# Transformer block on one core: the FFN of token-tile pairs computes silu and product for two inner blocks at once, under a new instruction order

## The chip, the core and the metric

The kernel runs on one core of a Trainium2 chip. The core has five engines with a queue each: TensorE (PE in the profile; its weight loads, which overlap the matmuls, are listed as PEld), VectorE (DVE), ScalarE (ACT), GpSimd (POOL) and SyncE (SP). SP issues nearly all DMA transfers here. The engines meet through semaphores. TensorE writes its results to PSUM, which has 8 banks of 512 fp32 columns by 128 partitions; DVE and ACT read them from there. The metric is the device time of one execution in microseconds, lower is better.

## The reference, cut to what matters

```python
x = A_x                                                # 1 x 2048 x 512, bf16
sa, ca, ga, sb, cb, gb = (silu(c) @ w_mod) in six parts of 512
h = layernorm(x) * (1 + ca) + sa
q, k, v = h @ wqkv, 32 heads of 16
# token s attends to tokens s, s-2, s-4, ..., s-14 (8 of them; those before 0 are masked)
x = x + ga * (softmax(q . k * 16**-0.5) weighted sum of v) @ wo
h = layernorm(x) * (1 + cb) + sb
x = x + gb * ((silu(h @ w1) * (h @ w3)) @ w2)          # 512 -> 1792 -> 512
```

The last line is the FFN, and the change is in it.

## The kernel before

**Tiles.** The 2048 tokens are 16 tiles of 128 (T = 0 to 15). All weights are loaded to SBUF once. Layernorm and the projections to q, k and v run over groups of 2, 2, 4, 4 and 4 tiles. v is written to a scratch tensor in DRAM and read back as eight shifted copies per tile (`vsh`, four DMAs a tile, into one of three buffers; the third, `vshx`, lies over the memory of `wqkv`, so it can be used only when all projections are done).

**Attention.** Per tile, DVE multiplies q with eight shifted views of k (line 742), TensorE sums these products into logits by small matmuls on a 128 x 32 tile of the array (line 752), DVE and ACT make the softmax, TensorE transposes the weights (line 807), DVE multiplies them with the shifted v (line 827), TensorE sums again by matmuls on a 128 x 32 tile (line 855), ACT copies the result (line 861), a DMA transposes it (`sb_ot`), TensorE multiplies it with wo (line 867), and DVE adds it to x (line 871).

**Second layernorm.** Sums of squares and the normalised tile are made on ACT (lines 590 and 601) with three small GpSimd instructions between them (lines 596 to 599). The first two groups of tiles are transposed on TensorE, the others by DMA (`sb_h`). ACT applies scale and shift (lines 644 and 621).

**FFN.** The tiles are taken in groups, `FFN = [[0,1],[2,3],[4,5,6,7],[8,9,10,11],[12,13],[14,15]]`. For a group, with `n` = 256 or 512 tokens, the inner width of 1792 is 14 blocks of 128. `ffn_unit` makes one block: 4 matmuls for the gate (w1) into one PSUM bank, silu on ACT into a buffer `tmp` (line 889), 4 matmuls for up (w3) into a second bank, and the product on DVE into a buffer `hh` (line 892). The matmuls of both are on line 883. For a pair of tiles, a block fills 256 of the 512 columns of each of its two banks. `ffn_w2` then takes the 14 `hh` blocks of a tile through w2 into one bank, 7 blocks and then 7 (line 921), or for the last two tiles in two halves of 256 columns, blocks 0 to 9 and then 10 to 13 (line 909); DVE adds x (line 931) and SP stores. w2 is first multiplied by gb on DVE in four groups of blocks (line 952).

**What sets the order.** `_build` lists operations with what they read and write. Each one's place is then fixed by two lists at the end of the file: `ORDER` gives the global order, from which every engine's own queue follows (SP's with its DMAs too), and `SLOTS` gives the PSUM bank or buffer of each value. Where an operation needs a value of another engine or of a DMA, or a buffer still held by an earlier value, its queue waits on a semaphore. Nothing is reordered at run time: a waiting operation holds all that follows on its engine. There are 20 `hh` buffers, 6 `tmp` buffers and 8 banks, shared by all stages. The costs `c_mm`, `c_act`, `c_dve` in the operations served the making of the lists, and do nothing in the running program.

Of the kernel before, what the change touches and what calls it, by code (L numbers as in the profile page):

```python
# [10 lines left out]
P = 128  # L11
# [261 lines left out]
def _build(p, A_x, A_wqkv, A_wo, B_w1, B_w3, B_w2, c, w_mod, out):  # L273
# [602 lines left out]
    def ffn_unit(gi, n, fi, vh, after):  # L876
        g = group_of[fi]
        k = ("f", NF * gi + fi)
        vgp, vup = Val("ps_g", psum), Val("ps_u", psum)

        def mm(e, vp, wt):
            for t in range(KT):
                ins = e.matmul(bank(vp)[:, 0:n], wt[:, t, fi * P:(fi + 1) * P], vh.at[:, t, 0:n], start=(t == 0),  # L883
                               stop=(t == KT - 1))
            return ins

        vt, vh_ = Val("tmp", tmppool), Val("hh", hhpool)
        o = p.op("pe", lambda e: mm(e, vgp, w1), 4 * c_mm(n), k, r=[vh, vw1[g]], w=[vgp], after=after)
        p.op("act", lambda e: e.activation(vt.at[:, 0:n], bank(vgp)[:, 0:n], ACT.Silu), c_act(n), k, r=[vgp], w=[vt],  # L889
             table="silu")  # L890
        p.op("pe", lambda e: mm(e, vup, w3), 4 * c_mm(n), k, r=[vh, vw3[g]], w=[vup], after=[o])
        p.op("dve", lambda e: e.tensor_tensor(vh_.at[:, 0:n], vt.at[:, 0:n], bank(vup)[:, 0:n], ALU.mult), c_dve(n), k,  # L892
             r=[vt, vup], w=[vh_])
        return vh_
# [4 lines left out]
    def ffn_w2(T, tt, vhh, zops):  # L899

        if T >= NT - 2:
            n = D // 2
            for q in range(2):
                vz = Val("ps_z", psum)
                o = None
                for a, c in ((0, 10), (10, NF)):
                    def mm(e, q=q, vz=vz, a=a, c=c):
                        for fi in range(a, c):
                            ins = e.matmul(bank(vz)[:, 0:n], vhh[fi].at[:, tt * P:(tt + 1) * P], w2[:, fi, q * n:(q + 1) * n],  # L909
                                           start=(fi == 0), stop=(fi == NF - 1))  # L910
                        return ins

                    o = p.op("pe", mm, (c - a) * c_mm(n), ("z", 2 * T + q), r=vhh[a:c] + vw2s[0 if a == 0 else 2:3 if a == 0 else 4], part=[vz], after=[o] if o else [])
                store(T, q * n, n, vz)
            return
        vz = Val("ps_z", psum)
        o = None
        for q in range(2):
            def mm(e, q=q):
                for fi in range(7 * q, 7 * q + 7):  # L920
                    ins = e.matmul(bank(vz), vhh[fi].at[:, tt * P:(tt + 1) * P], w2[:, fi, :], start=(fi == 0),  # L921
                                   stop=(fi == NF - 1))
                return ins

            o = p.op("pe", mm, 7 * MM, ("z", 2 * T + q), r=vhh[7 * q:7 * q + 7] + vw2s[2 * q - (q > 0):2 * q + 2], part=[vz], after=[o] if q else [])
            zops[q].append(o)
        store(T, 0, D, vz)
# [34 lines left out]
    zold = []  # L962
    for gi, Ts in enumerate(FFN):
        vns = [v for pr in pairs(Ts) for v in ln_sums(pr)]
        vh = ln_T(1, gi, vns)
        spare = NHH - NF
        vhh = [ffn_unit(gi, len(Ts) * P, fi, vh, zold if fi < spare else zops[0] if fi < spare + 7 else zops[1]) for fi in range(NF)]
        zold, zops = zops[1], [[], []]
        for tt, T in enumerate(Ts):
            ffn_w2(T, tt, vhh, zops)  # L970
# [106 lines left out]
```

## Time and profile before

| | us |
|---|---|
| median of 3 runs | 239.71 (237.94 to 240.3) |
| the profiled execution: its time | 239.43 |
| its span, first to last instruction | 237.7 |
| PE busy | 229.7 (97%) |
| DVE busy | 179.4 (75%) |
| ACT busy | 138.5 (58%) |
| POOL busy | 29.2 (12%) |
| DMA, share of 16 engines | 67% |
| FFN gate and up matmuls (line 883), busy | 53.0 with 256 columns, 49.9 with 512 |
| FFN down matmuls (lines 921 and 909), busy | 44.0 and 6.3 |

How to read it: a busy time is the union of an engine's instruction times. Matmuls are pipelined, so a matmul's row is longer than the step to the next one, and a TensorE that is busy by its rows may still have lost part of that time; where the text speaks of a step, it is the distance of the starts. A few matmul records are missing in the trace (25 of those on lines 691, 711, 867, 883 and 921). A line of a group gives engine, operation, output <- input, shapes and count, then busy time, mean duration in ns, and the engine's idle time before these instructions with what ended it. A line of the order in time gives start, duration, engine, line, operation and, in brackets, the idle time before it. `sb_hh` is `hh`, `sb_sg` is `tmp`, `pall` is PSUM, `sb_w` stands for w1, w2 and w3 together.

### The profile page before, as it was taken

To read this page: it belongs to the slowest core of one execution; us is meant where nothing else is said; L and a number is where in the kernel's file an instruction comes from. 1 tells how busy PE (TensorE), PEld (TensorE's weight loads), DVE (VectorE), ACT (ScalarE), POOL (GpSimd) and SP (SyncE) were. 2 spreads that over 40 slices of the span, in tenths; PEclk is the share of its full clock that TensorE was granted. 3 is DMA by queue.
4 is the path that set the end of the run, shared out by engine and by line. 5 is a ranking of instruction groups with operands and counts; after the bars stand their busy time and mean duration, and the time that the engine had idled before them with its cause. 6 is when DMAs were issued, how large, how long until landed. Compare 5 with 4: busy or idle time off the path is not lost.

```text
span 237.7 us, 4535 instructions
## 1 busy us (share of the span) xinstructions
PE 229.7 (97%) x1781; PEld 136.2 (57%) x1806; DVE 179.4 (75%) x279; ACT 138.5 (58%) x267; POOL 29.2 (12%) x66
## 2 busy tenths in 40 slices
PE   7999999999999998999999999999999999999995
PEld 4776454445588674664444444444475457485774
DVE  5699999999999989999999999682654403434433
ACT  2289577999978744985865594837473405040300
POOL 4434100013002000240002520012010000000000
PEclk9999999999999999999999999999999999999999
DMA  6999999999999999897981693642203000000202
GB/s 216 372 337 322 158 237 299 208 269 283 353 200 270 243 249 199 173 260 177 247 234 47 182 234 72 154 132 46 67 19 91 3 0 0 6 19 0 70 0 88
DMA packets 46317, 38.85 MB, mean 163 GB/s; under 512 B 21704, under 2 KB 37080, under 8 KB 46296
## 3 DMA queue, kind: packets, MB, share of 16 engines
q1 hardware_dynamic: 46288, 38.56, 66.9%
q8 instruction: 14, 0.23, 0.4%
q14 instruction: 7, 0.06, 0.1%
q10 hardware_dynamic: 8, 0.00, 0.0%
HBM read 29.62 MB, written 4.21 MB: 142 GB/s over the span
## 4 chain that ended last, share of the span: by engine, by line
PE 74%; DMA 8%; DVE 8%; SPq 4%; ACT 3%; issue 2%; ACTq 0%; DVEq 0%
PE pall L883 38%; PE pall L921 18%; DMA sb_x<-in_A_x_dram 5%; PE pall L867 5%; SPq L124 4%; PE pall L691 4%; DMA sb_vsh<-v_scratch_dram 3%; PE pall L909 3%; PE pall L855 2%; PE pall L752 2%; PE pall L711 2%; DVE sb_vsh L827 2%; DVE sb_pq L742 2%; DVE sb_hh L892 1%; ACT sb_h L621 1%
## 5 line engine op out<-in xcount | busy, mean ns | idle before, releaser
L883 PE MATMUL pall<-sb_h,sb_w 128*128 128x256 bf16 (+1 forms) x664 | 101.9, 307 | 1.8 <-DVE sb_hh L892 0.9
L883 PEld LDWEIGHTS pall<-sb_h,sb_w 128*128 128x128 bf16 x672 | 64.8, 98 | 37.2 <-issue 2.8
L889 ACT ACTIVATE sb_sg<-pall 128x256 bf16<-128x256 f32 (+1 forms) x84 | 35.6, 453 | 54.1 <-PE pall L883 53.0
L892 DVE TENSOR_TENSOR sb_hh<-sb_sg,pall 128x256 bf16<-128x256 bf16 (+1 forms) x84 | 39.9, 505 | 34.8 <-PE pall L883 32.7
L921 PE MATMUL pall<-sb_w,sb_hh 128*128 128x512 bf16 x190 | 44.0, 379 | 0.3
L742 DVE TENSOR_TENSOR sb_pq<-sb_q,sb_kT 128x4096 bf16<-128x4096 bf16 x16 | 36.3, 2282 | 0.0
L921 PEld LDWEIGHTS pall<-sb_w,sb_hh 128*128 128x128 bf16 x196 | 19.0, 98 | 21.6 <-DVE sb_hh L892 0.4
L691 PE MATMUL pall<-sb_h,sb_wqkv 128*128 128x512 bf16 (+1 forms) x154 | 30.2, 335 | 0.5 <-issue 0.2
L827 DVE TENSOR_TENSOR sb_vsh<-sb_vsh,sb_al 128x4096 bf16<-128x4096 bf16 x12 | 27.3, 2287 | 2.1 <-DMA sb_vsh<-v_scratch_dram 2.1
L621 ACT ACTIVATE sb_h<-sb_h,sb_modc 128x512 bf16<-128x512 bf16 (+1 forms) x24 | 16.5, 743 | 10.1 <-DMA sb_h<-sb_xn 10.1
L691 PEld LDWEIGHTS pall<-sb_h,sb_wqkv 128*128 128x128 bf16 x160 | 14.7, 98 | 11.8 <-ACT sb_ac L861 0.4
L931 DVE TENSOR_TENSOR sb_o<-pall,sb_x 128x512 bf16<-128x512 f32 (+1 forms) x18 | 11.1, 625 | 10.5 <-PE pall L921 6.8
L711 PE MATMUL pall<-sb_wqkv,sb_h 128*128 128x512 bf16 x62 | 15.5, 379 | 0.2
L867 PE MATMUL pall<-sb_wo,sb_ot 128*128 128x512 bf16 x61 | 15.3, 379 | 0.3 <-issue 0.2
L586 POOL TENSOR_SCALAR sb_nm<-sb_sx 128x2 f32<-128x2 f32 x8 | 1.7, 218 | 105.2 <-DVE sb_x L871 105.1
L644 ACT ACTIVATE sb_h<-pall,sb_modc 128x256 bf16<-128x256 bf16 (+1 forms) x18 | 9.9, 612 | 7.5 <-DVE sb_modc L509 6.5
L861 ACT ACTIVATE sb_ac<-pall 128x512 bf16<-128x512 f32 x16 | 9.5, 595 | 7.2 <-PE pall L855 7.1
L601 ACT ACTIVATE sb_xn<-sb_x,sb_nb,sb_rs 128x512 bf16<-128x512 bf16 x16 | 12.4, 806 | 0.7 <-POOL sb_nb L599 0.6
L871 DVE SCALAR_TENSOR_TENSOR sb_x<-pall,sb_x 128x512 bf16<-128x512 f32 x16 | 10.9, 686 | 1.5 <-PE pall L867 1.3
L590 ACT ACTIVATE sb_xn<-sb_x,sb_nm 128x512 bf16<-128x512 bf16 x16 | 11.4, 714 | 0.7 <-POOL sb_nm L586 0.7
L721 ACT ACTIVATE sb_v<-pall 128x512 bf16<-128x512 f32 x16 | 9.5, 600 | 2.8 <-PE pall L711 2.8
L555 DVE BATCH_NORM_STATS2 sb_st<-sb_x 128x6 f32<-128x512 bf16 x16 | 10.6, 680 | 0.8 <-DMA sb_x<-in_A_x_dram 0.7
(87 smaller groups left out, 208.3 us busy)
## 6 DMA issues: line engine op xcount, KB each, us to landing
sb_vsh<-v_scratch_dram SPq DMA_DIRECT2D x48, 256.0 KB, 5.5
sb_vshx<-v_scratch_dram SPq DMA_DIRECT2D x16, 256.0 KB, 4.6
sb_w<-in_B_w_dram SPq DMA_DIRECT2D x6, 512.0 KB, 7.9
sb_w<-in_B_w_dram SPq DMA_DIRECT2D x6, 384.0 KB, 5.4
v_scratch_dram<-sb_v SPq DMA_DIRECT2D x16, 128.0 KB, 6.4
out_dram<-sb_o SPq DMA_DIRECT2D x14, 128.0 KB, 1.8
sb_wqkv<-in_A_wqkv_dram SPq DMA_DIRECT2D x6, 256.0 KB, 6.3
sb_x<-in_A_x_dram SPq DMA_DIRECT2D x4, 256.0 KB, 6.4
```

What stands on the lines that cost most here:

```text
L590: p.op("act", lambda e, vn=vn, T=T: e.activation(vn.at[:], x_sb[:, T, :], ACT.Square, bias=nm[:, T, :], accum_out=var[:, T, :]), c_act(512 ...
L601: p.op("act", lambda e, vn=vn, T=T: e.activation(vn.at[:], x_sb[:, T, :], ACT.Identity, bias=nb[:, T, :], scale=rs[:, NT + T, :]), c_act(5 ...
L621: return e.activation(vh.at[:, ft, 0:n * P], vh.at[:, ft, 0:n * P], ACT.Identity, bias=modc[:, 8 * which + ft:8 * which + ft + 1], scale=m ...
L691: ins = e.matmul(bank(vp)[:, j * n:(j + 1) * n], wqkv[:, t, col:col + P], vh.at[:, t, 0:n], start=(t == ORDER[0] and j == 0), stop=(t == O ...
L711: ins = e.matmul(bank(vp), vh.at[:, t, tt * P:(tt + 1) * P], wqkv[:, t, 2 * D:3 * D], start=(t == ORDER[0]), stop=(t == ORDER[-1]))
L742: return e.tensor_tensor(vp.at[:], in0, in1, ALU.mult)
L827: return e.tensor_tensor(v_w, v_w, a_w, ALU.mult)
L867: ins = e.matmul(bank(vy), vt.at[:, ft, :], wo[:, ft, :], start=(ft == 0), stop=(ft == KT - 1))
L883: ins = e.matmul(bank(vp)[:, 0:n], wt[:, t, fi * P:(fi + 1) * P], vh.at[:, t, 0:n], start=(t == 0), stop=(t == KT - 1))
L889: p.op("act", lambda e: e.activation(vt.at[:, 0:n], bank(vgp)[:, 0:n], ACT.Silu), c_act(n), k, r=[vgp], w=[vt], table="silu")
L892: p.op("dve", lambda e: e.tensor_tensor(vh_.at[:, 0:n], vt.at[:, 0:n], bank(vup)[:, 0:n], ALU.mult), c_dve(n), k, r=[vt, vup], w=[vh_])
L921: ins = e.matmul(bank(vz), vhh[fi].at[:, tt * P:(tt + 1) * P], w2[:, fi, :], start=(fi == 0), stop=(fi == NF - 1))
```

## The change

For groups of two tiles, `ffn_unit` takes two blocks at a time (`m = 4 // len(Ts)`): 8 gate matmuls write the two halves of one bank, one silu reads 512 columns, 8 up matmuls write the two halves of a second bank, and one product of 512 columns is written to one `hh` buffer, of which each block is a half. For groups of four tiles nothing changes (`m` is 1). So the four pair groups have 7 units each in place of 14, 28 silus and 28 products fewer in all, and no matmul more or less. `ffn_w2` reads the halves, and for tiles 0 to 3, 12 and 13 its two parts are 8 and 6 blocks in place of 7 and 7. The program has 1006 operations in place of 1118. `ORDER` and `SLOTS` are new: the order is the same for the first 390 operations (on TensorE, until the logits of tile 6), and different from there, also for the attention, the loads of the weights, the reads of shifted v and the stores. The v projections of tiles 12 and 13 and some bank numbers of the part ahead of it change places as well.

```diff
-    def ffn_unit(gi, n, fi, vh, after):
-        g = group_of[fi]
-        k = ("f", NF * gi + fi)
+    def ffn_unit(gi, n, fis, vh, after):
+        k = ("f", NF * gi + fis[-1])
+        m = len(fis)
         vgp, vup = Val("ps_g", psum), Val("ps_u", psum)
+        gs = sorted({group_of[fi] for fi in fis})
 
         def mm(e, vp, wt):
-            for t in range(KT):
-                ins = e.matmul(bank(vp)[:, 0:n], wt[:, t, fi * P:(fi + 1) * P], vh.at[:, t, 0:n], start=(t == 0),
-                               stop=(t == KT - 1))
+            for j, fi in enumerate(fis):
+                for t in range(KT):
+                    ins = e.matmul(bank(vp)[:, j * n:(j + 1) * n], wt[:, t, fi * P:(fi + 1) * P], vh.at[:, t, 0:n],
+                                   start=(t == 0 and j == 0), stop=(t == KT - 1 and j == m - 1))
             return ins
...
-        p.op("act", lambda e: e.activation(vt.at[:, 0:n], bank(vgp)[:, 0:n], ACT.Silu), c_act(n), k, r=[vgp], w=[vt],
+        p.op("act", lambda e: e.activation(vt.at[:, 0:m * n], bank(vgp)[:, 0:m * n], ACT.Silu), c_act(m * n), k, r=[vgp], w=[vt],
              table="silu")
...
-        p.op("dve", lambda e: e.tensor_tensor(vh_.at[:, 0:n], vt.at[:, 0:n], bank(vup)[:, 0:n], ALU.mult), c_dve(n), k,
+        p.op("dve", lambda e: e.tensor_tensor(vh_.at[:, 0:m * n], vt.at[:, 0:m * n], bank(vup)[:, 0:m * n], ALU.mult), c_dve(m * n), k,
              r=[vt, vup], w=[vh_])
-        return vh_
+        return [(vh_, j * n) for j in range(m)]
...
-        for q in range(2):
-            def mm(e, q=q):
-                for fi in range(7 * q, 7 * q + 7):
-                    ins = e.matmul(bank(vz), vhh[fi].at[:, tt * P:(tt + 1) * P], w2[:, fi, :], start=(fi == 0),
-                                   stop=(fi == NF - 1))
+        for q, (a, c) in enumerate(((0, half), (half, NF))):
+            def mm(e, a=a, c=c):
+                for fi in range(a, c):
+                    ins = e.matmul(bank(vz), hh(fi), w2[:, fi, :], start=(fi == 0), stop=(fi == NF - 1))
                 return ins
...
-        vhh = [ffn_unit(gi, len(Ts) * P, fi, vh, zold if fi < spare else zops[0] if fi < spare + 7 else zops[1]) for fi in range(NF)]
+        m = 4 // len(Ts)
+        half = 6 + m
+        units = [list(range(fi, min(fi + m, NF))) for fi in range(0, NF, m)]
+        vhh = [x for i, fis in enumerate(units) for x in ffn_unit(gi, len(Ts) * P, fis, vh, freed[i])]
...
 ORDER = [
...
-    389, 390, 607, 609, 608, 337, 278, 315, 392, 313, 314, 322, 325, 445, 225, 338, 615, 610, 614, 616, 394, 611, 393, 613, 612,
...
+    278, 315, 392, 313, 314, 322, 325, 445, 225, 338, 615, 610, 614, 616, 394, 443, 611, 612, 305, 405, 617, 328, 272, 444, 326,
...
 ]
```

More of the change, by code (lines that the diff above doesn't have):

```diff
@@ L885, in mm @@
             return ins
         vt, vh_ = Val("tmp", tmppool), Val("hh", hhpool)
-        o = p.op("pe", lambda e: mm(e, vgp, w1), 4 * c_mm(n), k, r=[vh, vw1[g]], w=[vgp], after=after)
-        p.op("act", lambda e: e.activation(vt.at[:, 0:n], bank(vgp)[:, 0:n], ACT.Silu), c_act(n), k, r=[vgp], w=[vt],
+        o = p.op("pe", lambda e: mm(e, vgp, w1), 4 * m * c_mm(n), k, r=[vh] + [vw1[g] for g in gs], w=[vgp], after=after)
+        p.op("act", lambda e: e.activation(vt.at[:, 0:m * n], bank(vgp)[:, 0:m * n], ACT.Silu), c_act(m * n), k, r=[vgp], w=[vt],
@@ L890, in ffn_unit @@
              table="silu")
-        p.op("pe", lambda e: mm(e, vup, w3), 4 * c_mm(n), k, r=[vh, vw3[g]], w=[vup], after=[o])
-        p.op("dve", lambda e: e.tensor_tensor(vh_.at[:, 0:n], vt.at[:, 0:n], bank(vup)[:, 0:n], ALU.mult), c_dve(n), k,
+        p.op("pe", lambda e: mm(e, vup, w3), 4 * m * c_mm(n), k, r=[vh] + [vw3[g] for g in gs], w=[vup], after=[o])
+        p.op("dve", lambda e: e.tensor_tensor(vh_.at[:, 0:m * n], vt.at[:, 0:m * n], bank(vup)[:, 0:m * n], ALU.mult), c_dve(m * n), k,
@@ L893, in ffn_unit, with ffn_w2, hh, vals @@
              r=[vt, vup], w=[vh_])
-        return vh_
+        return [(vh_, j * n) for j in range(m)]
     finals = []
     zops = [[], []]
-    def ffn_w2(T, tt, vhh, zops):
+    def ffn_w2(T, tt, vhh, half, zops):
+        def hh(fi):
+            v, c = vhh[fi]
+            return v.at[:, c + tt * P:c + (tt + 1) * P]
+        def vals(a, c):
+            return list({id(v): v for v, _ in vhh[a:c]}.values())
+        def w2s(a, c):
+            return vw2s[group_of[a]:group_of[c - 1] + 1]
         if T >= NT - 2:
@@ L908, in mm @@
                         for fi in range(a, c):
-                            ins = e.matmul(bank(vz)[:, 0:n], vhh[fi].at[:, tt * P:(tt + 1) * P], w2[:, fi, q * n:(q + 1) * n],
+                            ins = e.matmul(bank(vz)[:, 0:n], hh(fi), w2[:, fi, q * n:(q + 1) * n],
                                            start=(fi == 0), stop=(fi == NF - 1))
                         return ins
-                    o = p.op("pe", mm, (c - a) * c_mm(n), ("z", 2 * T + q), r=vhh[a:c] + vw2s[0 if a == 0 else 2:3 if a == 0 else 4], part=[vz], after=[o] if o else [])
+                    o = p.op("pe", mm, (c - a) * c_mm(n), ("z", 2 * T + q), r=vals(a, c) + w2s(a, c), part=[vz], after=[o] if o else [])
                 store(T, q * n, n, vz)
@@ L917, in ffn_w2 @@
         o = None
-        for q in range(2):
-            def mm(e, q=q):
-                for fi in range(7 * q, 7 * q + 7):
-                    ins = e.matmul(bank(vz), vhh[fi].at[:, tt * P:(tt + 1) * P], w2[:, fi, :], start=(fi == 0),
-                                   stop=(fi == NF - 1))
+        for q, (a, c) in enumerate(((0, half), (half, NF))):
+            def mm(e, a=a, c=c):
+                for fi in range(a, c):
+                    ins = e.matmul(bank(vz), hh(fi), w2[:, fi, :], start=(fi == 0), stop=(fi == NF - 1))
                 return ins
-            o = p.op("pe", mm, 7 * MM, ("z", 2 * T + q), r=vhh[7 * q:7 * q + 7] + vw2s[2 * q - (q > 0):2 * q + 2], part=[vz], after=[o] if q else [])
+            o = p.op("pe", mm, (c - a) * MM, ("z", 2 * T + q), r=vals(a, c) + w2s(a, c), part=[vz], after=[o] if q else [])
             zops[q].append(o)
@@ L961, in _build @@
                 values(T, i, val)
-    zold = []
+    freed = [[] for _ in range(NHH)]
     for gi, Ts in enumerate(FFN):
@@ L965, in _build @@
         vh = ln_T(1, gi, vns)
-        spare = NHH - NF
-        vhh = [ffn_unit(gi, len(Ts) * P, fi, vh, zold if fi < spare else zops[0] if fi < spare + 7 else zops[1]) for fi in range(NF)]
-        zold, zops = zops[1], [[], []]
+        m = 4 // len(Ts)
+        half = 6 + m
+        units = [list(range(fi, min(fi + m, NF))) for fi in range(0, NF, m)]
+        vhh = [x for i, fis in enumerate(units) for x in ffn_unit(gi, len(Ts) * P, fis, vh, freed[i])]
+        freed = freed[len(units):]
+        zops = [[], []]
         for tt, T in enumerate(Ts):
-            ffn_w2(T, tt, vhh, zops)
+            ffn_w2(T, tt, vhh, half, zops)
+        freed += [zops[0]] * (half // m) + [zops[1]] * (len(units) - half // m)
     p.late = list(late.values())
```

116 rows, old and new, of tables (ORDER, SLOTS) are left out of this document.

## The prediction

> **What bounds the kernel now.** I read the busy time by stretches first, then TensorE in order of time, then the waits. The granted clock is 1.00 throughout, so TensorE's rate is the same in every row.
>
> ```profile
> 80.00:90.00 10.00, 9.13 (x99) 6.44 (x88) 8.82 (x9) 4.31 (x11) 0.00 (x0) 1.00 1.17 239
> 90.00:100.00 10.00, 9.59 (x70) 5.19 (x70) 9.86 (x19) 7.49 (x14) 0.62 (x4) 1.00 0.80 183
> ...
> 210.00:220.00 10.00, 9.95 (x73) 6.97 (x72) 4.38 (x10) 1.92 (x5) 0.00 (x0) 1.00 0.00 0
> ```
>
> (Columns: stretch, length, busy PE, weight loads, DVE, ACT, POOL, clock, DMA share, GB/s.) PE is full nearly everywhere; DVE too, until about 150 us. The DMA engines are full until about 90 us.
>
> ```profile
> 85.72 3.23 PE L883 MATMUL pall<-sb_h,sb_w 128*128 128x256 bf16 x28
> 89.82 1.05 PE L883 MATMUL pall<-sb_h,sb_w 128*128 128x256 bf16 x8 [0.87 <-DVE sb_hh L892]
> ...
> 93.19 0.61 PE L855 MATMUL pall<-sb_vsh,sb_ind 128*32 128x512 bf16 x8 [0.36 <-DVE sb_vsh L827]
> ```
>
> ```profile
> PE pall L883 <- DVE sb_hh L892: 0.9, 1, 0.9
> ...
> DVE sb_vsh L827 <- DMA sb_vsh<-v_scratch_dram: 2.1, 3, 1.0
> ```
>
> Here PE does stand still, and the second view says why: DVE waits 1.0 us for tile 7's shifted v (in place at 87.1), and the product that frees a PSUM bank comes after it.
>
> **How much could go.** The orders first differ on PE at 59.83 us. Behind it PE has, in both kernels, 504 matmuls of 256 columns at 0.109 us (6.28 us for 56), 476 of 512 columns at 0.216 (FFN 224 + 196, output projection 56), 24 tiled groups at 0.43, and 2.6 us of transposes and one v projection: 54.9 + 102.8 + 10.3 + 2.6 = 170.6 us. It ends at 235.0, so only 235.0 - 59.8 - 170.6 = 4.6 us is not work. By the starts of its instructions 1.9 us of that is three waits (0.30 at 63.9, 1.03 at 89, 0.53 at 93) and 2.1 us is 22 changes between tiled and full-size matmuls at 0.095; the new order has 20. So the gain is at most about 2.1 us (0.9%).
>
> **Products and silus.** 56 of each become 28.
>
> ```profile
> L892 DVE TENSOR_TENSOR sb_hh<-sb_sg,pall 128x256 bf16<-128x256 bf16 x56 | 21.8, 417 | 25.2 <-PE pall L883 24.9
> L889 ACT ACTIVATE sb_sg<-pall 128x256 bf16<-128x256 f32 x56 | 20.1, 382 | 35.9 <-PE pall L883 35.5
> ...
> L892 DVE TENSOR_TENSOR sb_hh<-sb_sg,pall 128x512 bf16<-128x512 bf16 x28 | 18.5, 682 | 9.6 <-PE pall L883 7.8 <-ACT sb_sg L889 1.7
> L889 ACT ACTIVATE sb_sg<-pall 128x512 bf16<-128x512 f32 x28 | 15.8, 597 | 18.2 <-PE pall L883 17.6 <-DVE sb_hh L892 0.5
> ```
>
> ```profile
> 75.43 2.12 DVE L892 TENSOR_TENSOR sb_hh<-sb_sg,pall 128x256 bf16<-128x256 bf16 x6
> ...
> 142.30 1.87 DVE L892 TENSOR_TENSOR sb_hh<-sb_sg,pall 128x512 bf16<-128x512 bf16 x3
> ```
>
> The durations overlap, so I count by runs: (2.12 - 0.41)/5 = 0.34 us a product of 256 columns, (1.87 - 0.68)/2 = 0.60 of 512. A pair saves 2 x 0.34 - 0.60 = 0.08 us; 28 pairs 2.2 us on DVE, half of it (1.1) before 110 us, where DVE is full, the rest where it idles 5 us in 10. ACT saves less than 0.1 x 28 and, since the exponentials of tile 6 now come ahead of the first silu, two table loads of 1.28; ACT is 58% busy, so I count nothing. The Trainium skill, "Perfetto Trace Analysis", section "Optimizing Scalar/DVE Operations", gives about 125 ns of fixed cost for DVE on PSUM: 28 x 0.125 = 3.5 us, an estimate above the 2.2 of the rows. The same section says that breaking instructions up may help where the engine is not saturated but makes others wait, which would speak against the change in the last 80 us.
>
> **Bank release.** A gate or up result of two blocks holds one bank and frees it once. Bounds: 14 x 2 fewer bank turns in two groups may save up to the 0.9 us wait on sb_hh; or each last product may come one half later, 0.3 us (0.60 - 0.34) at each of the 28, 8 us if all were on PE's path. I read each bank's next user off the slot list: in the tail the nearest release (up 5.6+7, then products 5.6+7 and 4.6+7, then gate 4.12+13) has 2.6 us of PE work over 1.3 us of DVE. I take 0.
>
> **The new order, up to the first output projections.** What the old wait at 89 needed goes: the load of w2's first group (512 KB) and tile 12's v store now stand behind tile 7's and 6's v loads on SP, so these land some 1.7 us earlier. But three w3/w1 loads and a quarter of tile 5's v load now stand ahead of tile 3's transposed attention output:
>
> ```profile
> 62.01 1.23 SPq L124 DMA_TRANSPOSE sb_ot<-sb_ac x1
> ...
> 64.45 1.78 SPq L124 DMA_TRANSPOSE sb_ot<-sb_ac x1
> ```
>
> ```profile
> DMA to landing us min/median/max: 5.0/5.9/6.9
> ```
>
> ```profile
> 63.10 0.60 PE L855 MATMUL pall<-sb_vsh,sb_ind 128*32 128x512 bf16 x8
> ...
> 70.05 0.81 PE L867 MATMUL pall<-sb_wo,sb_ot 128*128 128x512 bf16 x3
> ```
>
> (SP's issues; time from issue to landing of these two; PE's accumulation of tile 2 and output projection of tile 3.) It lands at 62.01 + 5.0 = 67.0, so the old projection at 70.05 never waited. DMAs on this queue land in the order of issue here, one upon the other: 384 KB loads 1.2 us apart, 512 KB 1.3, 256 KB of v 1.1, 128 KB 0.4. New ahead of it: 2 x 1.2 + 1.1, gone 1.3: it lands at 69.2. PE is there sooner than before, because the v projection of tile 12 (0.86 us) is moved behind it: DVE's product of tile 2 ends at 60.31 + 0.4 (tile 9's v store, now ahead of its data) + 2.29 = 63.0; then accumulation 0.43, five FFN halves of 8 x 0.109, transposes 0.22, a mode change 0.1: 68.1. **PE waits 1.1 us**, and all the FFN work behind it in its queue waits too. Tile 2's output lands 0.5 to 1.4 later, its projection ends at 71.0 to 71.4. DVE (after 63.0 seven softmax steps of 0.6, a product of 2.2, one of the FFN: 69.9) has that tile's residual add next, ahead of three products of the FFN and the 2.2 us product of tile 8, and waits as long. So the stall at 89 is traded for one at 68.
>
> **From there to the end.** From that projection to the first gate matmul of tiles 4 to 7 PE has 40.8 us of work (22 FFN halves 19.2, the down projection of four tiles 12.1, ten tiled groups 4.3, four output projections 3.5, the v projection and transposes 1.7) and 8 mode changes (0.8): 112.6 to 113.0; the old one starts at 113.07. That gate needs its normalised input: in the old run 12.5 us from the end of tile 6's residual add (99.64) to the last modulation (112.1), 1.3 of it one slow GpSimd instruction. The new add ends at 71.2 + 28.7 + 0.6 + 0.7 = 101.2, so the input is there at 112.4 to 113.7. The gate starts at 113.1, as before. DVE reaches the end of tile 8's product 38.2 us after its wait (nine attention products 19.8, 13 of the FFN 7.8, w2's scaling 4.0, softmax 3.0, six residual adds 3.6), at 109.5, when PE needs it at 110.9. Behind the gate both orders have 121.0 us on PE and 8 mode changes; the old one took 121.95. Tile 14's v load sits behind waits of up to 5 us on SP, but DVE idles there. Tile 7's now goes to the buffer that lies on wqkv and so waits for the moved v projection, until some 73 us; the queue ahead of it is then 5 us or more deep, so it costs nothing. The last matmuls are now a half of tile 15 in place of tile 14: the same add (0.42) and store. End of PE 235.05; add and store as now 2.7; outside the span 239.43 - 237.7 = 1.73: **239.5**, and 0.1 for crossings that are level by the sums (tile 6's product ends 0.06 us ahead of its accumulation). I forecast **239.6**. The profiled 239.43 is 0.1% below the median of the three runs, 239.71.
>
> **Rivals.**
> (A) The transposed outputs come in time and the old stall is gone as well: the gate waits for its input alone, 111.5 to 112.2, so 237.8 to 238.7, say 238.2. For it: 5.0 us is a loaded queue's time; later transposes in the trace land 2.4 us after issue. Against: at 62 us every DMA share is 9. The Trainium skill, "DMA: Bandwidth & Descriptors", section "Queues, rings and completion order", says that completion is not in order of issue within one issuing engine; by that rule A would hold. Here landings kept the order of issue between 57 and 90 us.
> (B) Slower: DVE becomes the bound between 70 and 110 us. The place is the accumulation of tile 6, whose product stands level with it; a pair's product behind a 2.2 us attention product holds its bank longer, and any DVE wait over 0.1 us beyond PE's own goes to PE one to one. If the v loads of tiles 7 and 6 (1.0 and 0.3 us of waits now), the last w2 scale (its load is issued at some 97 us, needed at 102) or a bank behind the product of tile 8 (2.2) cost it 1.5 to 4.5 us, the result is 241 to 244, say 242.5. For it: DVE is busy 9.9 of 10; against: it has 1.1 us less to do.
> (C) The pair's instruction is not cheaper than two: 28 x 0.08, 1.1 us of it before 110, passed to PE: 240.6. The 512-column rows speak against it.
>
> **How the numbers follow.** Measurements of this kernel (237.94 to 240.3) can't tell less than about 1% from no change. Forecast 0.54 (238.7 to 240.8, all within 1%), A 0.23 (a quarter of it below 237.3, where faster by over 1% begins), B 0.20 (three quarters above 242.1, where slower by over 1% begins), C 0.03. So faster 0.06, slower 0.15, same 0.79. The range 237.5 to 242.4 leaves out 0.07 of A and 0.12 of B.
>
> **What would show it.** Right: 28 products and 28 silus of 512 columns more and none of 256; no PE wait near 89; a PE wait of about 1 us ahead of the first output projection near 68, ended by the DMA of sb_ot, and DVE waiting on it near 70; the first 512-column gate matmul near 113; from there 122 us. Wrong: no wait on sb_ot (A), or PE waiting for sb_vsh, sb_hh or DVE's scaled w2 between 73 and 110 (B), or waits in the last 80 us, where I have found none.

## The result and the profile after

The changed kernel takes 249.16 us (median of 4 runs, 248.43 to 252.32) against 239.26 for the kernel before in the same comparison: a ratio of 1.0415, 95% interval 1.0363 to 1.0468. The forecast was 239.6, with a range to 242.4. The profiled execution took 248.48, its span is 246.7, and PE's last instruction ends at 244.16 in place of 235.02. So 9.1 us have to be found on PE.

PE by stretches (columns as before: length, busy PE, weight loads, DVE, ACT, POOL, clock, DMA share, GB/s):

```profile
60.00:70.00 10.00, 7.86 (x101) 5.91 (x100) 9.60 (x11) 7.38 (x13) 0.00 (x0) 1.00 1.25 247
70.00:80.00 10.00, 8.47 (x69) 6.45 (x71) 7.44 (x10) 5.02 (x11) 3.28 (x4) 1.00 1.07 254
80.00:90.00 10.00, 10.00 (x122) 8.44 (x120) 9.02 (x11) 7.94 (x13) 0.00 (x0) 1.00 0.75 182
90.00:100.00 10.00, 9.95 (x92) 6.67 (x92) 9.98 (x11) 4.82 (x9) 1.25 (x1) 1.00 0.95 196
100.00:110.00 10.00, 9.95 (x47) 4.53 (x47) 9.51 (x12) 4.93 (x11) 5.26 (x7) 1.00 0.96 227
110.00:120.00 10.00, 5.05 (x63) 2.35 (x61) 8.11 (x8) 4.06 (x6) 2.87 (x2) 1.00 0.40 97
120.00:130.00 10.00, 9.55 (x40) 4.15 (x41) 5.24 (x6) 7.38 (x11) 0.00 (x0) 0.83 0.95 218
```

The stretch from 80 to 100, where the old kernel stood still near 89 and 93, is now full. PE loses time in three other places: in the first two stretches, above all between 110 and 120, and behind that by a granted clock of 0.83 (the mean of a part at 1.00 and a part at half). The waits say for what (waiter <- releaser: us in total, times, longest):

```profile
ACT sb_xn L590 <- POOL sb_nm L586: 9.9, 6, 3.6
...
ACT sb_xn L601 <- POOL sb_nb L599: 8.0, 3, 5.7
...
PE pall L885 <- ACT sb_h L621: 5.2, 1, 5.2
...
PE pall L867 <- DMA sb_ot<-sb_ac: 2.4, 1, 2.4
...
PE pall L636 <- ACT sb_xn L601: 1.1, 1, 1.1
```

In order of time: PE waits 2.6 us (start to start) near 68 for tile 3's transposed output, 1.26 near 78 for the normalised tiles 2 and 3, and 5.4 at 114.8 for the input of tiles 4 to 7 (`sb_h`), made by ACT. ACT itself waits for GpSimd: 9.9 and 8.0 us on lines that wait 0.7 and 0.6 in the old run. GpSimd is busy 34.9 us in place of 29.2. GpSimd and DVE in order of time, for tiles 4 to 7:

```profile
98.75 2.19 POOL L586 TENSOR_SCALAR sb_nm<-sb_sx 128x2 f32<-128x2 f32 x1 [20.12 <-DVE sb_x L871]
102.58 0.19 POOL L596 TENSOR_SCALAR sb_rs<-sb_var 128x2 f32<-128x2 f32 x1 [1.64 <-ACT sb_xn L590]
102.85 0.71 POOL L597 TENSOR_TENSOR sb_rs<-sb_rs,sb_cst 128x2 f32<-128x2 f32 x1
103.64 0.20 POOL L599 TENSOR_TENSOR sb_nb<-sb_nm,sb_rs 128x2 f32<-128x2 f32 x1
103.80 0.22 POOL L586 TENSOR_SCALAR sb_nm<-sb_sx 128x2 f32<-128x2 f32 x1
106.88 1.66 POOL L596 TENSOR_SCALAR sb_rs<-sb_var 128x2 f32<-128x2 f32 x1 [2.86 <-ACT sb_xn L590]
108.63 2.63 POOL L597 TENSOR_TENSOR sb_rs<-sb_rs,sb_cst 128x2 f32<-128x2 f32 x1
111.33 1.62 POOL L599 TENSOR_TENSOR sb_nb<-sb_nm,sb_rs 128x2 f32<-128x2 f32 x1
```

```profile
98.58 2.29 DVE L742 TENSOR_TENSOR sb_pq<-sb_q,sb_kT 128x4096 bf16<-128x4096 bf16 x1
...
106.21 2.29 DVE L742 TENSOR_TENSOR sb_pq<-sb_q,sb_kT 128x4096 bf16<-128x4096 bf16 x1
108.41 2.29 DVE L827 TENSOR_TENSOR sb_vsh<-sb_vsh,sb_al 128x4096 bf16<-128x4096 bf16 x1
110.61 2.28 DVE L827 TENSOR_TENSOR sb_vshx<-sb_vshx,sb_al 128x4096 bf16<-128x4096 bf16 x1
```

The same instruction on 128 x 2 numbers takes 0.22 us at 103.80 and 2.19 at 98.75; L596 takes 0.19 or 1.66, L597 0.71 or 2.63, L599 0.20 or 1.62. Each long one falls beside an attention product of DVE that reads both its inputs from SBUF, and ends when that product ends (98.75 + 2.19 = 100.94 against 98.58 + 2.29 = 100.87), or 0.56 later for L597, whose own work is 0.70 (111.26 against 110.70). One that starts first keeps its length: in the old run a power on line 597 starts at 53.03, 0.28 us ahead of a product, and takes 0.71 us, and the product takes its 2.28. Between 70 and 120 us the old order has one long instruction, and it too stands beside a product (before):

```profile
100.83 2.28 DVE L742 TENSOR_TENSOR sb_pq<-sb_q,sb_kT 128x4096 bf16<-128x4096 bf16 x1
...
101.65 1.52 POOL L596 TENSOR_SCALAR sb_rs<-sb_var 128x2 f32<-128x2 f32 x1 [0.70 <-ACT sb_xn L590]
```

Near 78 of the run after there is one more of this kind (2.19 at 73.55, beside q by k of tile 8).

So the sum by PE's starts: 2.6 near 68 with 0.3 for a late accumulation near 62, 1.3 near 78, 5.4 near 115, and 1.6 because the first eight 512-column matmuls behind that stall step 427 ns in place of 216: 11.2 in all. The old waits (1.9) and two mode changes (0.2) are gone: +9.1. From the first gate matmul of tiles 4 to 7 to the end it is 123.7 us, the old 121.95 and the 1.6 of slow clock.

The new products and silus are there as said (28 more of 512 columns, none of 256):

```profile
L894 DVE TENSOR_TENSOR sb_hh<-sb_sg,pall 128x512 bf16<-128x512 bf16 x56 | 36.9, 683 | 35.5 <-PE pall L885 31.9
L891 ACT ACTIVATE sb_sg<-pall 128x512 bf16<-128x512 f32 x56 | 31.8, 594 | 46.3 <-PE pall L885 45.1
```

### The profile page after: what moved, and what is told of

Read it like the earlier page. It is cut to its first block, busy times and chain, and to the rows that moved or that the text cites. A ratio compares the mean times of both kernels' runs of the same rounds, so it can differ in the third digit from the quotient of the medians.

```text
span 246.7 us, 4471 instructions
## 1 busy us (share of the span) xinstructions
PE 231.9 (94%) x1782; PEld 137.4 (56%) x1806; DVE 177.1 (72%) x251; ACT 132.7 (54%) x237; POOL 34.9 (14%) x66
## 4 chain that ended last, share of the span: by engine, by line
PE 50%; DMA 1%; ACT 1%; issue 0%; SPq 0%; DVE 0%
PE pall L885 30%; PE pall L933 12%; PE pall L867 3%; PE pall L921 2%; DMA sb_h<-sb_xn 1%; ACT sb_h L621 1%; PE pall L855 1%; PE pall L752 1%; PE pall L807 0%; SPq L124 0%; DVE sb_o L942 0%
## 5 line engine op out<-in xcount | busy, mean ns | idle before, releaser
L894 DVE TENSOR_TENSOR sb_hh<-sb_sg,pall 128x512 bf16<-128x512 bf16 x56 | 36.9, 683 | 35.5 <-PE pall L885 31.9
L891 ACT ACTIVATE sb_sg<-pall 128x512 bf16<-128x512 f32 x56 | 31.8, 594 | 46.3 <-PE pall L885 45.1
L933 PE MATMUL pall<-sb_w,sb_hh 128*128 128x512 bf16 x190 | 43.3, 379 | 0.4 <-issue 0.2
L586 POOL TENSOR_SCALAR sb_nm<-sb_sx 128x2 f32<-128x2 f32 x8 | 5.7, 713 | 116.2 <-DVE sb_x L871 116.2
L827 DVE TENSOR_TENSOR sb_vshx<-sb_vshx,sb_al 128x4096 bf16<-128x4096 bf16 x4 | 9.1, 2285 | 3.4 <-DMA sb_vshx<-v_scratch_dram 3.4
L867 PEld LDWEIGHTS pall<-sb_wo,sb_ot 128*128 128x128 bf16 x64 | 6.0, 98 | 9.5 <-DMA sb_ot<-sb_ac 2.5
```

Source lines behind the costliest of these rows:

```text
L827: return e.tensor_tensor(v_w, v_w, a_w, ALU.mult)
L867: ins = e.matmul(bank(vy), vt.at[:, ft, :], wo[:, ft, :], start=(ft == 0), stop=(ft == KT - 1))
L891: p.op("act", lambda e: e.activation(vt.at[:, 0:m * n], bank(vgp)[:, 0:m * n], ACT.Silu), c_act(m * n), k, r=[vgp], w=[vt], table="silu")
L894: p.op("dve", lambda e: e.tensor_tensor(vh_.at[:, 0:m * n], vt.at[:, 0:m * n], bank(vup)[:, 0:m * n], ALU.mult), c_dve(m * n), k, r=[vt, v ...
L933: ins = e.matmul(bank(vz), hh(fi), w2[:, fi, :], start=(fi == 0), stop=(fi == NF - 1))
```

## The experiments

Three theories. **S**: the loss is GpSimd's small instructions held up by DVE's two-input products, with the late output near 68 as a term of its own. **W**: the wide silu and product, which hold a bank and a buffer for two blocks. **D**: late landings of DMAs, all else being their consequence.

### The new order without the wide instructions

```diff
-        p.op("act", lambda e: e.activation(vt.at[:, 0:m * n], bank(vgp)[:, 0:m * n], ACT.Silu), ...)
+        def silu(e):
+            for j in range(m):
+                ins = e.activation(vt.at[:, j * n:(j + 1) * n], bank(vgp)[:, j * n:(j + 1) * n], ACT.Silu)
+            return ins
...  # the product on DVE likewise
```

> The kernel after, with silu and product of a pair of blocks as two instructions of 256 columns each, in the same place of the same order. Theory S (stretched statistics: of the 9.1 us lost, 1.3 + 5.4 + 1.6 come from GpSimd's small instructions of the second layernorm that run beside DVE's products, and 2.6 from the late transposed output): width is not the cause, both PE waits stay (2 to 3 us near 68, 4 to 7 us near 115); 248 to 251. Rival W (the wide silu and product hold banks and buffers too long): most of the loss goes, 239 to 243.

Measured: 249.93 us, ratio 1.0411 (1.0367 to 1.0455), the same as after. PE's waits:

```profile
PE pall L885 <- ACT sb_h L621: 5.4, 1, 5.4
PE pall L867 <- DMA sb_ot<-sb_ac: 2.6, 2, 2.3
...
PE pall L636 <- ACT sb_xn L601: 1.1, 1, 1.1
```

All three are there. So the width of the instructions is not the cause of the loss under this order. The run leaves the other half of W in place: a pair still holds its bank and its buffer until the second instruction is done. For that half the waits after speak: PE waits for the transposed output, for normalised tiles and for `sb_h`, and none of its long waits is for a bank or an `sb_hh`. DVE is busy 178.6 us here and 177.1 after: 28 wide products save 1.5 us.

### The products in quarters

q by k of tiles 8, 10 and 11 and weights by v of tiles 8 and 9, each as four instructions:

```diff
-                return e.tensor_tensor(vp.at[:], in0, in1, ALU.mult)
+                w = W // PQ_IN.get(T, 1)              # PQ_IN = {8: 4, 10: 4, 11: 4}, AV_IN = {8: 4, 9: 4}
+                for a in range(0, W, w):
+                    in0 = ...  # the same views, w of the 8 shifts from a
+                    ins = e.tensor_tensor(vp.at[:, a:a + w], in0, in1, ALU.mult)
+                return ins
```

> The kernel after, with the five attention products that GpSimd's slow instructions ran beside (q by k of tiles 8, 10, 11 and weights by v of tiles 8 and 9) each as four instructions of a quarter of the size. Theory S: GpSimd comes between the quarters, its instructions take under 0.9 us in place of 1.6 to 2.6, the wait near 115 falls from 5.4 to under 1.5 us and the clock behind it stays at 1.0, the wait near 78 falls from 1.3 to under 0.4; 240 to 243, with the wait of 2.6 near 68 still there. Rivals W and D (late landings set the rest): 248 to 250, DVE being 0.9 us slower.

Measured: 245.07 us, ratio 1.0215 (1.0176 to 1.0254). GpSimd comes in between the quarters:

```profile
97.91 0.59 POOL L588 TENSOR_SCALAR sb_nm<-sb_sx 128x2 f32<-128x2 f32 x1 [20.34 <-DVE sb_x L879]
100.13 1.01 POOL L598 TENSOR_SCALAR sb_rs<-sb_var 128x2 f32<-128x2 f32 x1 [1.63 <-ACT sb_xn L592]
...
105.25 0.63 POOL L598 TENSOR_SCALAR sb_rs<-sb_var 128x2 f32<-128x2 f32 x1 [2.38 <-ACT sb_xn L592]
105.96 1.02 POOL L599 TENSOR_TENSOR sb_rs<-sb_rs,sb_cst 128x2 f32<-128x2 f32 x1
107.06 0.62 POOL L601 TENSOR_TENSOR sb_nb<-sb_nm,sb_rs 128x2 f32<-128x2 f32 x1
```

The wait near 78 falls from 1.26 to 0.28, the one near 115 from 5.4 to 2.5, and the clock of the profiled execution stays at 1.00 (the others have 0.99 and take 244.9 to 245.5 us). PE's last instruction ends 5.2 us sooner, though DVE has 15 instructions more. That is S in kind, 2 us short in size: 0.3 to 0.45 us per GpSimd instruction is left of the hold-up beside the quarters, 0.8 at 100.13 beside a scaling of w2 (0.95 us, both inputs in SBUF) that was not cut, and the last transpose of the four tiles lands at 113.8, 2.8 us after its issue ended (see the last section).

### The transposed outputs first

```diff
 SP's queue:
   w1_1
-  w3_3
   w2_1
-  w3_2
   v store of tile 7
-  shifted v of tile 5, a quarter
   transposed output of tile 3, of tile 2
+  w3_3, w3_2, shifted v of tile 5, a quarter
   w1_2
```

> The kernel after, with the loads of w3's third and fourth group and one quarter of tile 5's shifted v behind the transposed outputs of tiles 3 and 2 in SP's queue. Theory S: only the wait near 68 goes (2.6 to under 0.7 us), the one near 115 stays at 4 to 6 us; 245 to 247. Rival D (everything behind is late because of that output): 238 to 240.

Measured: 250.56 us, ratio 1.0450 (1.0418 to 1.0481). The outputs land in time, at 65.0 and 68.1, but PE then waits for a weight:

```profile
PE pall L885 <- ACT sb_h L621: 5.2, 1, 5.2
PE pall L885 <- DMA sb_w<-in_B_w_dram: 3.5, 1, 3.5
```

`w1_2` now lands at 75.4, PE needs it at 71.9. The expected time was missed, since these loads have no slack to give. The first line answers the question all the same: without the late output, the wait near 115 is unchanged. Alone it does not rule D out, as another late landing took the output's place (3.5 us for `w1_2`). Two other runs do: with the quarters the output is as late as before (PE waits 2.5 us for it) and the wait near 115 is halved, and in the next run it is gone with the output still late.

### GpSimd without reads

```diff
+        def stat(fn, out, value):
+            return (lambda e: e.memset(out, value)) if 2 <= Ts[0] <= 6 else fn
-        p.op("pool", lambda e: e.tensor_scalar(nm[:, i:i + n, 0], sx[:, i:i + n, 0], -1.0 / D, ...
+        p.op("pool", stat(lambda e: e.tensor_scalar(nm[:, i:i + n, 0], sx[:, i:i + n, 0], -1.0 / D, ...), nm[:, i:i + n, 0], 0.0), ...
...  # the other three likewise; order and slots are those of after
```

> The kernel after in the same order, but GpSimd's four instructions of the second layernorm of tiles 2 to 7 are memsets that read nothing (mean, variance, its power and the bias are left out for these tiles, so their normalised values are wrong). Theory S, by a conflict of GpSimd's reads of SBUF with DVE's two-input products: each takes under 0.3 us, the waits near 78 and 115 fall from 1.3 and 5.4 to under 0.3 and 1.5, no half clock, the 2.5 near 68 stays: 240.5 to 243. If the conflict is not in the reads (any GpSimd instruction beside such a product is held back), or the wait has another cause: 246 to 249.

Measured: 241.00 us (8 runs, 239.26 to 242.06), ratio 1.0073 (1.0040 to 1.0106). GpSimd in order of time, and PE's waits:

```profile
97.69 0.10 POOL L587 MEMSET sb_nm<- 128x2 f32 x1 [21.38 <-DVE sb_x L874]
...
104.14 0.26 POOL L587 MEMSET sb_rs<- 128x2 f32 x2 [1.61 <-ACT sb_xn L593]
104.45 0.10 POOL L587 MEMSET sb_nb<- 128x2 f32 x1
```

```profile
PE pall L870 <- DMA sb_ot<-sb_ac: 2.0, 1, 2.0
```

The memset at 97.69 stands where L586 took 2.19 us in the run after, directly behind the residual add of tile 4 and beside q by k of tile 11, and takes 0.10; the two at 104.14 run beside the scaling of w2 (103.49 to 104.44, both inputs in SBUF). The waits near 78 and 115 are gone, only the late output is left, and PE ends at 235.98, 8.2 us sooner. The half clock is gone too in the profiled execution (240.30 us); four of the eight have a mean clock of 0.99 and take 241.5 to 242.1 us. Some 0.9 us of the chain is owed to a memset being shorter than the instruction it replaces even undisturbed (0.10 to 0.13 against 0.19 to 0.70); the rest is the hold-up. This is S in its expected size. That it hangs on what GpSimd reads is the nearest reading; the run does not separate it from the memset being another kind of instruction. The Trainium skill, "SBUF — State Buffer", section "Who interferes with whom", has both halves: a DVE instruction with two SBUF inputs contends with a GpSimd instruction that reads SBUF, not with one that only writes it, and whoever issues first holds the shared port for its whole instruction. The traces agree: 2.19 against 0.10 us at the same place, and long ones that end with the product. They show only one side of it: DVE's products beside GpSimd keep their 2.28 or 2.29 us.

### One exchange on DVE, and repairs that keep the work

```diff
 DVE's queue:
   residual add of tile 5
+  residual add of tile 4
   product of blocks 2+3, tiles 2 and 3
-  residual add of tile 4
   q by k of tile 11
```

> The kernel after with two neighbours on DVE exchanged: the residual add of tile 4 now comes ahead of the product of the blocks 2+3 of the second pair group. So GpSimd's first instruction for tiles 4 and 5 starts some 0.6 us before DVE's next two-input product (q by k of tile 11) in place of with it. Theory S: that instruction takes 0.22 us again, squares and normalising on ACT come some 2 us sooner, and the later three GpSimd instructions fall largely beside other DVE work; the wait near 115 falls from 5.4 to 0.4 to 1.2 us and the half clock behind it goes: 242 to 244.5. Rival W (width): 248 to 250. Rival D (late landings): 248 to 250.

Measured: 246.91 us, ratio 1.0352 (1.0313 to 1.0392).

```profile
98.50 0.22 POOL L586 TENSOR_SCALAR sb_nm<-sb_sx 128x2 f32<-128x2 f32 x1 [19.88 <-DVE sb_x L871]
...
106.24 2.80 POOL L597 TENSOR_TENSOR sb_rs<-sb_rs,sb_cst 128x2 f32<-128x2 f32 x1
109.12 1.62 POOL L599 TENSOR_TENSOR sb_nb<-sb_nm,sb_rs 128x2 f32<-128x2 f32 x1
```

The first instruction is short, as expected. But the power of tiles 6 and 7 starts at 106.24, 0.04 us after q by k of tile 10 (106.20), and is held for all of it; the next one is held by the next product. The wait falls from 5.4 to 4.1 us only, and the half clock lasts longer (13 matmuls). The expectation missed by a crossing of 0.04 us.

The next two runs move more, with all work kept. The first has, besides the exchange, a shift of DMAs and of a w2 scaling:

```diff
 SP's queue:
-  w2_1 (behind w3_3); shifted v of tile 5, a quarter (behind the v store of tile 7)
   transposed output of tile 3, of tile 2
   w1_2
+  w2_1, shifted v of tile 5, a quarter
 DVE's queue:
   residual add of tile 3
+  scaling of w2_1
   q by k of tile 8
   product of blocks 6+7
-  scaling of w2_1
```

> The exchange of the run before, and two more repairs. On SP the load of w2's second group and one quarter of tile 5's shifted v go behind the transposed outputs of tiles 3 and 2 and w1's third group (w3's loads stay in place). On DVE the scaling of that w2 group goes directly behind the residual add of tile 3, ahead of the product q by k of tile 8, so that GpSimd's first instruction for tiles 2 and 3 runs beside 1.2 us and not 2.2. Theory S with the late landing as a separate term: the waits near 68 (2.5), 78 (1.3) and 115 (5.4 and 1.6 of half clock) fall to under 0.5, 0.6 and 1.0: 238.8 to 240.5, level with before. Rival W: 244 or more, since the width is unchanged.

Measured: 244.91 us, ratio 1.0264 (1.0230 to 1.0298). The wait near 68 is gone (0.2 us), which settles that term. The one near 78 grew to 2.5: the scaling waits 2.1 us for its load, so q by k of tile 8 comes later and now holds the power of tiles 2 and 3 (2.63 us at 74.95). Near 115 it is 3.4 us, again with L597 at 2.80. The hold-up had only been moved to other instructions.

The second has the exchange, q by k of tiles 8 and 10 in quarters, the w2_1 load and the quarter of v directly behind the transposed outputs, and on ACT:

```diff
 ACT's queue:
   squares of tiles 5 and 4
-  normalise tiles 5 and 4
   squares of tiles 7 and 6
+  normalise tiles 5 and 4
```

> The kernel after with four repairs, all work kept: on DVE the residual add of tile 4 ahead of the product of blocks 2+3; on ACT the normalising of tiles 4 and 5 behind the squares of tiles 6 and 7, so that the last GpSimd instructions come some 1.4 us sooner, beside DVE instructions that read PSUM; on SP the load of w2's second group and a quarter of tile 5's v behind the transposed outputs of tiles 3 and 2; and q by k of tiles 8 and 10 in four instructions each. Theory S and the late landing: waits near 68, 78 and 115 under 0.5, 0.4 and 1.5: 239 to 241. If width costs by itself: 243 or more.

Measured: 242.50 us, ratio 1.0151 (1.0106 to 1.0196). The last group's GpSimd instructions take 0.19, 0.70 and 0.32 us. What is left are two waits for DMAs: 1.7 us near 71 for w1_2, and 3.0 near 113. A last run puts w1_2 first and two small v stores behind the transposes:

```diff
 SP's queue:
   transposed output of tile 3, of tile 2
+  w1_2
   w2_1, shifted v of tile 5, a quarter
-  w1_2
...
   transposes of tiles 4, 5, 6, 7
+  v stores of tiles 14 and 12
   shifted v of tile 11
-  v stores of tiles 14 and 12
```

> The hand repairs with two changes on SP, for the two waits that they left (1.7 us near 71 for w1's third group, 3.0 near 113 where the transposed tile 7 landed 4.2 us after its issue began, beside the first load of tile 11's v, and not some 2.3): w1's third group goes directly behind the transposed outputs, ahead of w2's second group and the quarter of tile 5's v; and two small v stores (tiles 14 and 12) go between the transposes of tiles 4 to 7 and the loads of tile 11's v. Theory S and the late landing: both waits fall, the first under 0.4, the second under 1.5 us: 237.5 to 239.5, level with or up to 0.8% below before, with the wide units. If the width costs by itself, or the last landing does not depend on what stands behind it: 240.5 or more.

Measured: 242.65 us, ratio 1.0146 (1.0095 to 1.0197). The first wait is gone. The second stays at 3.0 us: tile 7's transpose is issued at 107.8 and lands at 112.1, what stands behind it makes no difference, and this half of the expectation fails. By the ratios (1.0415 to 1.0146) the repairs bring back some 6.4 of the 9.9 us, and no version with all work kept beats the kernel before.

### The wide instructions in the old order

```diff
 order: for each two blocks a, b of a pair group
-  gate a, silu a, up a, product a  and  gate b, silu b, up b, product b, each at its place
+  gate a+b, silu a+b, up a+b, product a+b, each at the old place of b's
 banks: the old one where it is free, else the one longest free
```

> The wide units in the old order: each pair of blocks stands where the second of the two stood, and the buffers are given out anew with the old ones preferred. Theory S: the wide unit costs nothing by itself, 238.5 to 241, and no GpSimd instruction of the second layernorm of tiles 4 to 7 but the one of before is stretched. Rival W: 244 or more.

Measured: 245.93 us, ratio 1.0267 (1.0238 to 1.0297). GpSimd is busy 28.9 us (29.2 before), with one long instruction between 70 and 120 us as in the old run, and yet PE ends 6.4 us later, against S's expectation. In order of time its waits are 1.9 us near 58 (a bank), 1.0 near 82, 1.1 near 94, 1.4 near 122 and 0.9 near 172, most of them for silus or accumulations whose bank now comes free later. The same order with the banks given out anew:

```diff
-  banks: the old one where it is free, else the one longest free
+  banks: the one longest free
```

> Again the wide units in the old order, but each PSUM bank goes to the buffer that has been free longest in the order, in place of the old bank where it was free. Theory S: most of the 6.3 us of the run with the old banks preferred were bank conflicts of that choice (1.9 near 58, 1.4 near 122, 1.1 near 94, 0.9 near 172); with them gone 240 to 242.5, the rest being pairs that wait for their second block. Rival W: as before, 244.5 to 247.

Measured: 242.74 us, ratio 1.0175 (1.0144 to 1.0207). Half of it was the choice of banks. The other half (PE ends 3.2 us later than before) is six waits of 0.3 to 1.0 us:

```profile
PE pall L855 <- DVE sb_vsh L827: 0.8, 1, 0.8
PE pall L885 <- DVE sb_x L871: 0.5, 2, 0.4
PE pall L933 <- DVE sb_w L963: 0.5, 1, 0.5
...
PE pall L933 <- DVE sb_hh L894: 0.3, 1, 0.3
```

So a pair in an order that was made for single blocks is not free: it costs 3.2 us with the better of the two choices of banks. The likely reason is that DVE's work of both blocks comes in one piece, and later than the first block's came; no run tried that by itself. W holds there, and no wait shows it under the new order, which was made with the pairs in it.

### Two searched orders

Both keep the wide instructions and were found by moving operations within their queues (373 values have another bank or buffer in the first run, 191 in the second) while running the queues with durations from the traces and with the hold-up of GpSimd as a rule. The first starts from the changed kernel, the second from the kernel with the hand repairs.

> The wide units under an order that was searched from the one of after, by running the queues with the durations of the traces, and with GpSimd's instructions held back for as long as a DVE product with both inputs in SBUF runs. Theory S: no PE wait over 0.5 us behind 60 us, 237.5 to 239.2, 0.3 to 0.8% below before. If width costs by itself (W) or something in the queues is missing: 241 or more.

> The run before with operations and buffers behind 60 us moved further by a search that runs the queues with the durations of the traces (landings and GpSimd's hold-ups varied); the first 60 us are left as they are, where the search of the earlier run had moved DMAs that its model times badly. Theory S: no PE wait over 0.5 us behind 62 us, 238 to 239.5, level with before or up to 0.4% below. If width or something else outside the model costs: 241 or more.

Measured: 258.58 us (ratio 1.0849, 1.0817 to 1.0882) and 247.87 (1.0377, 1.0341 to 1.0412). Both miss by far. In the first PE stands still 3.9 us between 50 and 60; in the second DVE waits 12.1 us for shifted v in all. The likely reason is that such a search leans on what its model times worst, here the landings of DMAs; that was not tried. The two runs say nothing for or against S.

## Why the prediction was wrong, step by step

**What bounds the kernel, how much could go.** Right: the waits at 63.9, 89 and 93 are gone, the gain could not be more than 2.1 us, and it was 1.9 and two mode changes.

**Products and silus.** Right: 2.2 us less DVE time was forecast; DVE is busy 2.3 us less than before, and 1.5 less than in the run with halves. ACT is busy 5.8 us less.

**Bank release, taken as 0.** Right under the new order, as far as the waits show: none of PE's long waits is for a bank. No run varied it there, since the run with halves holds banks as long. It is not a property of the pair: in the old order the same pairs cost 3.2 us of PE, and 6.4 with the first choice of banks.

**The output near 68.** The mechanism was right (with loads of weights and a quarter of v moved behind it, the wait is gone; the sum counts two w3 loads and the quarter, where the sentence ahead of it speaks of three loads). The mis-sized term is the landing: forecast 69.2, measured 70.17, so PE waits 2.6 and not 1.1 us. The transfers do land one upon the other, but the queue moved next to nothing from 68.7 to 69.9 (last section).

**From there to the gate: the step that failed.** "That gate needs its normalised input: in the old run 12.5 us from the end of tile 6's residual add (99.64) to the last modulation (112.1), 1.3 of it one slow GpSimd instruction." I carried this chain over as a duration of 11.2 to 12.5 us. It took 16.8 us, from 103.6 to 120.4: 1.4 to 2.0 us more on each of four GpSimd instructions, the first of them (98.75) by way of ACT, which did tiles 5 and 4 that much later and tiles 7 and 6 behind them. The end of the residual add moved too, from the forecast 101.2 to 103.6: the larger wait near 68 (1.5 us) and the one near 78, of the same cause, which I had not foreseen at all (1.3). The sign was in my hands: an instruction of 0.19 us that takes 1.52 in the old trace (101.65). I counted it as part of the chain, and did not ask what stood beside it and where the new order puts the others. With GpSimd's reads taken away, and some 0.9 us of its own work with them, the time is 241.0 us, inside the range.

**Behind the gate.** "Both orders have 121.0 us on PE": right, but the forecast took the clock as 1.00 throughout, and a stall of 5.4 us cost 1.6 more. The Trainium skill, "TensorE: Matmul & The Clock Gate", Part 1, gives half rate after an idle window of about 3.4 us and the same time of work to leave it; the stalls of 4.1 to 5.6 us here agree (8 to 14 matmuls at 427 ns, 3.4 to 6.0 us). Shorter waits do not sort by length: the last section has one of 2.5 us that half clock followed, and some of 3.0 to 3.4 that it did not.

**The rivals.** B had the right sign, but none of its prices was paid: no PE wait over 0.3 us between 80 and 113 us is for shifted v, a bank or w2's scaling. A and C are out: the output was late, and the wide product is cheaper. What was missing was a rival in which an engine that is 12% busy sets the end.

## What to carry to other kernels

Where GpSimd's small instructions stand in a chain to PE, their place beside DVE's long instructions with both inputs in SBUF counts for more than their own length: look in the trace for one instruction with two very different durations, and read what ran beside the long ones. A chain that an order is to keep must be timed anew from its parts, not carried over as a sum. If such a hold-up can't be ordered away, cutting the long products into quarters bounds it, at the price of a little DVE time.

## What the runs showed of the hardware that was not expected

**A GpSimd instruction of 0.2 us can take ten times that.** 0.19 to 0.22 us alone, 1.5 to 2.2 where it starts inside a product of 2.29; an instruction of 0.70 that starts 0.04 us behind the product took 2.80. Between two products in a row one GpSimd instruction comes in, and the next waits for the second product.

**The queue of transfers can stand still behind one packet of instructions.** The DMA view of 107 to 113 us of the last repaired kernel (40 slices of 0.15 us: busy share in tenths, GB/s; then packets, MB and share by kind), and of 66 to 72 us of after:

```profile
DMA  3000079950006089999600000000039899930076
GB/s 58 0 0 0 2 174 285 288 123 2 0 0 109 19 207 273 254 63 1 0 0 0 0 5 9 9 9 10 10 116 280 239 287 328 389 116 0 0 82 109
...
q8 instruction: 1, 0.02, 1.7%
```

```profile
DMA  9999999900000999990000000079939999969899
GB/s 232 229 220 212 191 147 89 44 27 27 27 9 19 195 266 273 231 22 0 0 2 7 9 10 10 9 202 379 364 92 312 343 312 328 460 218 437 259 218 218
...
q8 instruction: 1, 0.02, 1.1%
```

One packet of 0.02 MB occupies one of 16 engines for 1.7% of 16 x 6 us = 1.6 us (1.1 us in the second), and behind it the queue falls to 10 GB/s or less for eleven slices from 109.7 (eight from 68.7). The transfers under way land that much later: tile 3's output in after, the transpose of tile 7 in the run with quarters and in the two last repaired kernels. The old kernel has the same packet near 68 and a gap of 1.4 us behind it; there the transfers under way land late too, but PE takes the later of the two outputs only at 72.01. The packet is not enough by itself: one of the same size near 53 in after, near 84 in the old kernel and near 82 in the last repaired one leaves the transfers going at over 100 GB/s. Where they stop, a transposing DMA is under way each time. Whether it takes the two together no run has varied. That the packet is the cause is read off the coincidence in these traces; no run moved it.

**The half clock does not follow the length of a wait alone.** Waits of 3.0 us near 113 (in the last two repaired kernels) and 3.4 near 116 left the clock at 1.00, and one of 2.5 near 77 (in the run with the moved w2 scaling) was followed by it. The stretches at half clock in the traces last 3.41 or 6.83 us, and in a trace their edges lie whole steps of 3.41 us apart. Read by such steps, first the run with the moved w2 scaling, then the last repaired kernel (columns as before):

```profile
76.66:80.08 3.42, 1.33 (x15) 1.16 (x16) 3.42 (x5) 2.20 (x4) 1.11 (x2) 1.00 1.07 268
80.08:83.49 3.41, 3.41 (x40) 2.29 (x42) 2.21 (x3) 2.12 (x5) 0.00 (x0) 0.50 0.47 112
```

```profile
113.10:116.51 3.41, 1.46 (x7) 0.70 (x8) 2.19 (x1) 3.39 (x6) 0.00 (x0) 1.00 1.00 283
116.51:119.93 3.42, 3.42 (x18) 1.57 (x16) 2.01 (x4) 3.38 (x5) 0.00 (x0) 1.00 0.55 126
```

PE is busy for 39% of the first row and 43% of the third; half clock follows only the first. Over all traces of this case, ten such steps at full clock ahead of PE's last instruction have PE busy for 40% or less, and nine of them are followed by half clock (the exception is 1.25 of 3.42 us near 68, in the run with quarters); no step with 41% or more is. So where a wait falls against these steps counts. They lie differently in each execution, and one kernel shows different clocks: of six executions of the last repaired kernel two have a mean of 1.00 and four 0.99. No run moved a wait against the steps on purpose.

**Left open:** why the repaired kernels, with every GpSimd instruction of the last group under 0.8 us, still need 242.5 us; 3.0 of the 3.5 us over the kernel before stand in the one wait near 113, whose last transpose lands late, and four of the six executions of the last kernel have a stretch at half clock that the profiled one lacks.
